# Gated linear attention, top-1 experts and a dense ELU layer in one kernel: joined weight layouts, dense weights kept in SBUF, another order of the attention loop

## The chip, the cores and the metric

The kernel runs on one core of a Trainium2 chip. The metric is the device time of one execution in microseconds; it is given as the median of several runs. Beside it there is one execution recorded by the profiler, with a time and a span of its own.

## The reference

Three layers follow each other, all in fp32.

```python
y[t] = q[t] @ S[t];  S[t] = alpha[t][:, None] * S[t-1] + outer(k[t], v[t])   # 4 x 8 heads, 768 steps, D = 48
x = y regrouped to (3072, 384)
logits = normalize(x) @ normalize(expert_emb).T / tau
idx, gate = argmax(logits), softmax(logits)[argmax]                         # 8 experts
x = gate * (relu(x @ w1[idx]) @ w2[idx])                                    # 384 -> 1024 -> 384
h = x @ w_in                                                                # 384 -> 2048
out = where(h > 0, h, exp(min(h, 0)) - 1) @ w_out                           # 2048 -> 384
```

## The kernel before

All of it is one program with three stages; the order of the instructions is written out by hand, so each engine executes its queue in the order in which the code issues to it.

**Attention (0 to 196 us)** works on 24 tiles of 128 tokens (six time chunks of four batches). Per tile, `stA` (L304) computes on VectorE a backward scan `R` (L316) and a forward scan `A` (L325), each over 112x517 elements, and on GpSimd the products `Kh` = k times `R` (L321) and `Qh` = q times `A` (L328). `stT` transposes `Kh` on TensorE. `stB` (L343) makes the score matrices in PSUM and masks them on VectorE into `P` (L354, two instructions per tile, PSUM in, SBUF out). `stC` and `stD` are the output and state matmuls, `stG` (L384) takes the state update from PSUM (`G`, L391), `stH` loads and prepares what the next tiles need. The loop in `fast` (L603) runs these stages for different tiles in one pass; `mid` is run between the two scans of `stA`.

Routing goes in groups of four tiles: logits, maximum, one-hot, counts and positions are small VectorE instructions on 128x32 or smaller tiles (`stR1`, `stR2`, `stX`, `gates`), put into lists (`todo`, `urgent`) from which `step(n)` takes n at a time. When a tile's gate is known, `scale_x` (L510) scales its rows on ScalarE and `put` (L518) writes the token number beside them on GpSimd (L522) and scatters them to DRAM (`xs`, one region per expert) with an indirect DMA from GpSimd (L523). In twelve of the tiles one piece of an expert weight is split on the side: the high part `whi` by ScalarE (L175), the remainder `wlo` by VectorE (L178); a remainder that is still due waits in the list `lag` and is issued at the end of a pass. After the loop `ending` handles the last two tiles and groups.

**Experts, `moe1` (196 to 473 us)**: 8 experts of 8 blocks. A block n is 9 matmuls of the first layer (`mm1`, L876, weights w1) and 9 of the second for the block before (`mm2`, L890, weights w2), each with 432 columns and with weights and activations split into high and low parts (three products). VectorE and ScalarE form `hh` (L886) and `hl` (L887) of each block. Blocks 4 to 6 of an expert hold the transposes of the next expert's rows (`turn`, L852; L864 and L866). At block 6 of each expert SP issues `idl` (L930), the copy of that expert's token numbers, element by element, from `xs` to a list in DRAM. Expert weights come in 32 loads of 768 KB, each of three pieces that `split_piece` (L162) splits one at a time, with two raw buffers (`stage`) and a ring of 8 high and 8 low buffers of 128x1536.

Beside this, `moe1` prepares the weights of the dense layer, which arrive as 64-bit patterns. In 32 steps j, one to two blocks apart, `decode` (L205) turns a piece of 384 KB into 128x384 fp32 (three integer instructions on VectorE, L212 to L214, a Square on ScalarE, two on GpSimd), `decode_end` (L221) splits it a step later (ScalarE copy L226, VectorE subtraction L227) and writes both halves to DRAM through SP's queue, and `load_d(j + 2)` (L196, L200) fetches the next-but-one raw piece. In the last two experts `load_dense` (L232) reads the split halves back into the ring.

**Dense layer, `moe2` (473 to 882 us)**: 6 slices of 512 tokens by 16 blocks, 21 matmuls each; VectorE and ScalarE compute the ELU (`mn` L1032, `g` L1035, `gl` L1039) with three blocks of lag, and a scatter from GpSimd (L1061) writes the output.

Of the kernel before, what the change touches and what calls it, by code (L numbers as in the profile page):

```python
# [11 lines left out]
I32 = mybir.dt.int32  # L12
# [27 lines left out]
SLOT = 1536  # L40
XW = DM + 1
# [14 lines left out]
def fused_kernel(ctx, tc, qk, a, v, emb, w1, w2, wi, wo, cst, sel, cols, out):  # L56
# [5 lines left out]
    ring = ctx.enter_context(tc.tile_pool(name="ring", bufs=8))  # L62
    stage = ctx.enter_context(tc.tile_pool(name="stage", bufs=2))
# [76 lines left out]
    wq = []  # L140
    for e in range(E):
        for s in range(2):
            wq.append(("w1", e, s, w1[e, :, s * SLOT:(s + 1) * SLOT]))
        for s in range(2):
            wq.append(("w2", e, s, w2[e, :, s * SLOT:(s + 1) * SLOT]))
    raw, whi, wlo = {}, {}, {}
    nload = [0]

    def load_w(n=1):
        for _ in range(n):  # L150
            if nload[0] < len(wq):
                nm, e, s, src = wq[nload[0]]
                t = stage.tile([128, SLOT], F32, tag="raw", name="raw")
                nc.sync.dma_start(out=t, in_=src)
                raw[nload[0]] = t
                nload[0] += 1

    PIECES = 3
    pieces = [(i, j) for i in range(len(wq)) for j in range(PIECES)]
    npc = [0]  # L160

    def split_piece(lag=None):  # L162

        if npc[0] >= len(pieces):
            return
        i, j = pieces[npc[0]]
        npc[0] += 1
        nm, e, s, _ = wq[i]
        if j == 0:
            whi[nm, e, s] = ring.tile([128, SLOT], F32R, tag="whi", name="whi")  # L170
            wlo[nm, e, s] = ring.tile([128, SLOT], F32R, tag="wlo", name="wlo")
        w = SLOT // PIECES
        sl = slice(j * w, (j + 1) * w)
        h, l, r = whi[nm, e, s], wlo[nm, e, s], raw[i]
        nc.scalar.activation(out=h[:, sl], in_=r[:, sl], func=AF.Copy)  # L175

        def low_part():
            nc.vector.tensor_tensor(l[:, sl], r[:, sl], h[:, sl].bitcast(F32), op=ALU.subtract)  # L178
            if j == PIECES - 1:
                raw.pop(i)  # L180
                if i != AHEAD - 1:
# [10 lines left out]
    d_hi = {nm: dram.tile([128, 4 * SLOT], F32, name=nm + "_hi") for nm in ("wi", "wo")}  # L192
    d_lo = {nm: dram.tile([128, 4 * SLOT], F32, name=nm + "_lo") for nm in ("wi", "wo")}
    dbuf = {}
# [8 lines left out]
    dpart = {}  # L203

    def decode(j, pool):  # L205
        if j >= len(dq):
            return
        w = dbuf.pop(j).bitcast(I32).rearrange("p (n two) -> p n two", two=2)
        lo, hi = w[:, :, 0], w[:, :, 1]
        t = pool.tile([128, HS], I32, name="dt")  # L210
# [8 lines left out]
        dpart[j] = (g, tf)  # L219

    def decode_end(j):  # L221
        if j not in dpart:
            return
        nm, s, _ = dq[j]
        g, tf = dpart.pop(j)
# [12 lines left out]
    def wblk(nm, e, col, n):  # L238
        s, c0 = divmod(col, SLOT)
        return whi[nm, e, s][:, c0:c0 + n], wlo[nm, e, s][:, c0:c0 + n]  # L240
# [19 lines left out]
    def attention():  # L260
        with ExitStack() as st:
# [17 lines left out]
            ones = gp.tile([128, 1], F32, name="ones")  # L279

# [21 lines left out]
            Qh, Kh, Rs = {}, {}, {}  # L302

            def stA(i, mid):  # L304

# [4 lines left out]
                if i >= NT:  # L310
                    mid()
                    return
                al = at.pop(i)
# [12 lines left out]
                step(2)  # L326
# [843 lines left out]
```

## Time and profile before

| what | value |
| --- | --- |
| median of 3 runs | 892.02 us (891.55 to 892.13) |
| the profiled execution, its own time | 883.97 us |
| its span | 882.2 us |
| mean granted TensorE clock | 0.955 |
| TensorE busy | 819.9 us (93%) |
| VectorE busy | 565.3 us (64%) |
| ScalarE busy | 356.5 us (40%) |
| GpSimd busy | 207.8 us (24%) |
| HBM read, written | 81.68 MB, 24.81 MB |

How to read it: busy time is the time in which an engine executes, out of the whole span; a matmul is counted with a modelled end, so a busy TensorE isn't one at its peak. The granted clock is a share of TensorE's full speed. Views that are cut by a stretch of time show where an engine is busy and where it is not; a view of waits names the instruction that ended an idle time, in square brackets or behind an arrow.

### The profile page before, as it was taken

How to read it: one execution, taken by the hardware profiler on the slowest of the kernel's cores; microseconds unless marked ns; L12 is line 12 of the kernel's file. 1: busy time of each engine (PE TensorE's matmuls, PEld its weight loads, DVE VectorE, ACT ScalarE, POOL GpSimd, SP SyncE). 2: the span in 40 equal slices, each digit the busy share in tenths (PEclk: the TensorE clock that was granted, in tenths of full speed). 3: DMA queues.
4: the chain of work that ended last, by engine and by line, in shares of the span. 5: the costliest groups of instructions: out<-in, count | busy, mean ns of one | idle time of the engine just before them, and what ended most of it. 6: DMA issues, size and time to landing. Idle time of an engine off the chain costs nothing.

```text
span 882.2 us, 13140 instructions
## 1 busy us (share of the span) xinstructions
PE 819.9 (93%) x4880; PEld 736.4 (83%) x4880; DVE 565.3 (64%) x1054; ACT 356.5 (40%) x739; POOL 207.8 (24%) x235
## 2 busy tenths in 40 slices
PE   7999888749997988989999999999999999999995
PEld 5888777629986987978988999999999999999995
DVE  7899999935785676867734555555555555555552
ACT  2556654614453454545523333333333333333331
POOL 6435555531233233323431001101100100100102
PEclk7898888978998999999999999999999999999999
DMA  9977795235888778978999000000000000000000
GB/s 265 311 191 192 205 261 158 55 102 184 198 241 189 183 223 208 243 208 209 307 299 214 1 1 10 27 1 9 27 1 9 29 1 4 33 0 1 37 1 36
DMA packets 47554, 107.50 MB, mean 122 GB/s; under 512 B 11880, under 2 KB 26472, under 8 KB 47472
## 3 DMA queue, kind: packets, MB, share of 16 engines
q1 hardware_dynamic: 42096, 84.46, 36.0%
q0 software_dynamic: 5376, 22.04, 7.9%
q8 instruction: 41, 0.67, 0.3%
q14 instruction: 41, 0.34, 0.1%
HBM read 81.68 MB, written 24.81 MB: 121 GB/s over the span
## 4 chain that ended last, share of the span: by engine, by line
PE 62%; DMA 8%; DVE 4%; issue 1%; ACT 1%; SPq 0%; POOLq 0%; POOL 0%; DVEq 0%; ACTq 0%
PE h L1030 22%; PE o L1052 8%; PE o L1050 8%; PE o L1051 8%; DMA wi_lo<-dt 5%; DMA wo_lo<-dt 3%; PE y L897 3%; PE y L896 3%; PE y L898 3%; PE h L881 2%; PE h L883 2%; PE h L882 2%; DVE wlo L178 1%; DVE hl L887 1%; PE t L864 1%
## 5 line engine op out<-in xcount | busy, mean ns | idle before, releaser
L1033 ACT ACTIVATE mn<-mn 128x512 f32<-128x512 f32 x96 | 60.7, 632 | 182.4 <-DVE mn L1032 182.4
L1052 PE MATMUL o<-whi,gl 128*128 128x384 f32 x384 | 129.3, 337 | 0.0
L1050 PE MATMUL o<-whi,gh 128*128 128x384 f32 x384 | 129.3, 337 | 0.0
L1051 PE MATMUL o<-wlo,gh 128*128 128x384 f32 x384 | 129.1, 336 | 0.0
L1030 PE MATMUL h<-xh,whi 128*128 128x512 f32 x288 | 112.5, 391 | 0.6 <-ACT x2T L910 0.6
L1030 PE MATMUL h<-xh,wlo 128*128 128x512 f32 x288 | 113.0, 393 | 0.0
L1039 DVE TENSOR_TENSOR gl<-g,gh 128x512 fp32r<-128x512 f32 x96 | 66.6, 694 | 72.4 <-ACT gh L1038 72.4
L1030 PE MATMUL h<-xl,whi 128*128 128x512 f32 x288 | 112.9, 393 | 0.0
L1035 DVE SCALAR_TENSOR_TENSOR g<-mn,h 128x512 f32<-128x512 f32 x96 | 66.1, 689 | 72.6 <-ACT mn L1033 72.6
L1061 POOL DMA_INDIRECT out_dram<-ob,ids x24 | 23.7, 986 | 363.3 <-DVE gl L1039 243.8
L1038 ACT ACTIVATE gh<-g 128x512 fp32r<-128x512 f32 x96 | 60.7, 632 | 77.8 <-DVE g L1035 77.0
L1032 DVE TENSOR_SCALAR mn<-h 128x512 f32<-128x512 f32 x96 | 66.2, 690 | 37.4 <-PE h L1030 37.1
L896 PE MATMUL y<-hh,whi 128*128 128x432 f32 x192 | 73.3, 382 | 9.8 <-ACT hh L886 7.8
L897 PE MATMUL y<-hl,whi 128*128 128x432 f32 x192 | 71.8, 374 | 7.9 <-DVE hl L887 7.9
L178 DVE TENSOR_TENSOR wlo<-raw,whi 128x512 fp32r<-128x512 f32 x96 | 75.6, 810 | 3.8 <-ACT whi L175 3.8
L217 POOL TENSOR_SCALAR dg<-dg 128x384 f32<-128x384 f32 x32 | 41.4, 1293 | 151.6 <-ACT dg L216 151.6
L1050 PEld LDWEIGHTS o<-whi,gh 128*128 128x128 f32 x384 | 72.1, 188 | 3.9
L1051 PEld LDWEIGHTS o<-wlo,gh 128*128 128x128 f32 x384 | 72.1, 188 | 3.8
L1052 PEld LDWEIGHTS o<-whi,gl 128*128 128x128 f32 x384 | 72.1, 188 | 0.0
L898 PE MATMUL y<-hh,wlo 128*128 128x432 f32 x192 | 70.7, 368 | 0.0
L881 PE MATMUL h<-xh,whi 128*128 128x432 f32 x192 | 70.4, 367 | 0.0
L883 PE MATMUL h<-xh,wlo 128*128 128x432 f32 x192 | 69.9, 364 | 0.0
(205 smaller groups left out, 1542.4 us busy)
## 6 DMA issues: line engine op xcount, KB each, us to landing
raw<-in_w_dram SPq DMA_DIRECT2D x32, 768.0 KB, 5.2
qk<-in_qk_dram SPq DMA_DIRECT2D x24, 448.0 KB, 8.1
vt<-in_v_dram SPq DMA_DIRECT2D x24, 352.0 KB, 6.8
raw<-in_wi_dram SPq DMA_DIRECT2D x16, 384.0 KB, 4.1
raw<-in_wo_dram SPq DMA_DIRECT2D x16, 384.0 KB, 4.6
at<-in_alpha_dram SPq DMA_DIRECT2D x24, 226.2 KB, 7.2
xr<-xs SPq DMA_DIRECT2D x7, 576.0 KB, 11.2
wi_hi<-dg SPq DMA_DIRECT2D x16, 192.0 KB, 5.8
```

The source lines that it names most:

```text
L178: nc.vector.tensor_tensor(l[:, sl], r[:, sl], h[:, sl].bitcast(F32), op=ALU.subtract)
L881: nc.tensor.matmul(ps, wh, xh[:, kk], start=(kk == 0), stop=False)
L883: nc.tensor.matmul(ps, wl, xh[:, kk], start=False, stop=(kk == KD - 1))
L896: nc.tensor.matmul(acc[e][d], wh, hh, start=(f == 0), stop=False)
L897: nc.tensor.matmul(acc[e][d], wh, hl, start=False, stop=False)
L898: nc.tensor.matmul(acc[e][d], wl, hh, start=False, stop=(f == FB - 1))
L1030: nc.tensor.matmul(ps, l, x, start=(n == 0), stop=(n == len(terms) - 1))
L1032: nc.vector.tensor_scalar(mn, ps, 0.0, None, op0=ALU.min)
L1039: nc.vector.tensor_tensor(gl, g, gh.bitcast(F32), op=ALU.subtract)
L1050: nc.tensor.matmul(o_, gh[:, sl], wh, start=(f == 0), stop=False)
L1051: nc.tensor.matmul(o_, gh[:, sl], wl, start=False, stop=False)
L1052: nc.tensor.matmul(o_, gl[:, sl], wh, start=False, stop=(f == M - 1))
```

## The change

1. **One weight layout.** w1 and w2 are interleaved on the host into `w12`, 768 columns for each block of an expert. Raw weights are loaded piece by piece (128x512) into six buffers, and each split of a piece issues one more load. The ring has 4 buffers of each kind instead of 8.
2. **Dense weights stay in SBUF.** `decode` writes into a pool `dense` of 18 tiles of 128x768; `decode_end`, the DRAM tensors and `load_dense` are gone. `split_dense` splits one block of a weight into ring buffers (high part) and `dense` tiles (low part): six pairs in the last blocks of `moe1`, the others in the first pass of `moe2`. `load_d(j + 1)` stands ahead of `decode(j)`.
3. **Buffers.** `xr` has a pool of its own; the split input of `moe2` is held in one tile per 128 rows instead of one for all 384.
4. **Attention's order.** `stA` is taken apart: scan `R`, reciprocal and `Kh` (`stR`), then the two `P` (`stP`; its matmuls, `stS`, go ahead), then the scatter of a tile (`put`), then scan `A` and `Qh` (new `stA`), then `G`, the logits, five routing steps, a weight remainder, seven more routing steps. The token number is written by ScalarE in `scale_x`; a `memset` of one element stands ahead of the scatter on GpSimd. The two chains of `stR1` are interleaved two to one.

The diff, cut to its core:

```diff
-    ring = ctx.enter_context(tc.tile_pool(name="ring", bufs=8))
-    stage = ctx.enter_context(tc.tile_pool(name="stage", bufs=2))
+    ring = ctx.enter_context(tc.tile_pool(name="ring", bufs=4))
+    stage = ctx.enter_context(tc.tile_pool(name="stage", bufs=2 * PIECES))
...
+    pieces = [(e, s, j) for e, s in wq for j in range(PIECES)]
...
+                t = stage.tile([128, PW], F32, tag="raw", name="raw")
+                nc.sync.dma_start(out=t, in_=w12[e, :, s * SLOT + j * PW:s * SLOT + (j + 1) * PW])
...
+            nc.vector.tensor_tensor(l[:, sl], r, h[:, sl].bitcast(F32), op=ALU.subtract)
+            load_w()
...
-    HS = SLOT // 4
+    HS = DM
...
+        d, r = divmod(s * HS, DS)
+        if r == 0:
+            dec[nm, d] = dense.tile([128, DS], I32, tag="wd", name="wd")
+        t = dec[nm, d][:, r:r + HS]
...
-    def decode_end(j):
-        nc.scalar.activation(out=g.bitcast(F32R), in_=tf, func=AF.Copy)
-        nc.vector.tensor_tensor(tf, tf, g, op=ALU.subtract)
-        sl = slice(s * HS, (s + 1) * HS)
-        nc.sync.dma_start(out=d_hi[nm][:, sl], in_=g)
-        nc.sync.dma_start(out=d_lo[nm][:, sl], in_=tf)
-    def load_dense(nm, s):
-        whi[nm, 0, s] = ring.tile([128, SLOT], F32R, tag="whi", name="whi")
-        wlo[nm, 0, s] = ring.tile([128, SLOT], F32R, tag="wlo", name="wlo")
-        nc.gpsimd.dma_start(out=whi[nm, 0, s], in_=d_hi[nm][:, s * SLOT:(s + 1) * SLOT])
-        nc.gpsimd.dma_start(out=wlo[nm, 0, s], in_=d_lo[nm][:, s * SLOT:(s + 1) * SLOT])
...
+    def split_dense(nm, m, dense):
+        if m >= F2 // 128:
+            return
+        s, c0 = divmod(m * DM, SLOT)
+        d, r0 = divmod(m * DM, DS)
+        if c0 == 0:
+            dhi[nm, s] = ring.tile([128, SLOT], F32R, tag="whi" if nm == "wi" else "wlo", name="d" + nm)
+        if r0 == 0:
+            dlo[nm, d] = dense.tile([128, DS], F32R, tag="wd", name="dlo")
+        h, l = dhi[nm, s][:, c0:c0 + DM], dlo[nm, d][:, r0:r0 + DM]
+        r = dec[nm, d][:, r0:r0 + DM].bitcast(F32)
+        nc.scalar.activation(out=h, in_=r, func=AF.Copy)
+        nc.vector.tensor_tensor(l, r, h.bitcast(F32), op=ALU.subtract)
+        if r0 + DM == DS:
+            dec.pop((nm, d))
...
+            def stR(i):
...
                 R = Rs[i] = wk.tile([C2, SW], F32, name="R")
-                A = wk.tile([C2, SW], F32, name="A")
-                nc.vector.tensor_tensor_scan(R[:, ::-1], al[:, ::-1], back[:, ::-1], 0.0, op0=ALU.mult, op1=ALU.max)
-                fo = fore[i % 2]
-                nc.vector.reciprocal(seg(fo)[:, :, 0:1], seg(R)[:, :, 1:2])
-                x = qkt.pop(i)
+                nc.vector.tensor_tensor_scan(R[:, ::-1], at[i][:, ::-1], back[:, ::-1], 0.0, op0=ALU.mult, op1=ALU.max)
+                nc.vector.reciprocal(seg(fore[i % 2])[:, :, 0:1], seg(R)[:, :, 1:2])
                 Kh[i] = wk.tile([C2, NP, T], F32, name="Kh")
-                nc.gpsimd.tensor_tensor(Kh[i], x[:, 1], R[:, 1:].rearrange("c (p t) -> c p t", t=TP)[:, :, 1:], op=ALU.mult)
-                step(2)
-                if i < NT - 2:
-                    mid()
-                nc.vector.tensor_tensor_scan(A, al, fo, 0.0, op0=ALU.mult, op1=ALU.add)
-                step(2)
+                nc.gpsimd.tensor_tensor(Kh[i], qkt[i][:, 1], R[:, 1:].rearrange("c (p t) -> c p t", t=TP)[:, :, 1:], op=ALU.mult)
...
+            def stA(i):
...
+                A = As[i] = wk.tile([C2, SW], F32, name="A")
+                nc.vector.tensor_tensor_scan(A, at.pop(i), fore[i % 2], 0.0, op0=ALU.mult, op1=ALU.add)
                 Qh[i] = wk.tile([C2, NP, T], F32, bufs=3, name="Qh")
-                nc.gpsimd.tensor_tensor(Qh[i], x[:, 0], seg(A)[:, :, 1:], op=ALU.mult)
-                nc.scalar.activation(out=chk[:, i], in_=seg(A)[:, :, 0:TP:T], func=AF.Copy)
-                if i >= NT - 2:
-                    mid()
+                nc.gpsimd.tensor_tensor(Qh[i], qkt.pop(i)[:, 0], seg(A)[:, :, 1:], op=ALU.mult)
...
+            def stP(i):
...
+                for h2, s in enumerate(sc.pop(i)):
+                    nc.vector.tensor_tensor(P[i][:, h2], s, c["tri"][:, None, :].to_broadcast([128, NP, T]), op=ALU.mult)
...
+                nc.scalar.activation(out=x[:, DM:], in_=c["tok"][:, i:i + 1], func=AF.Copy)
...
-                nc.gpsimd.tensor_copy(x[:, DM:], c["tok"][:, i:i + 1])
+                if apart and puts:
+                    nc.gpsimd.memset(tick, 0.0)
...
+                    stS(i + 1)
                     stT(i + 1)
-                    def mid():
...
-                    stA(i + 2, mid)
-                    if putq and i >= tail - 2:
+                    stR(i + 2)
+                    stP(i + 1)
+                    if putq and place[putq[0]][0] in gated:
                         put(putq.pop(0))
-                    stB(i + 1)
+                    stA(i + 2)
+                    stG(i - 1)
+                    while late:
+                        late.pop(0)()
+                    if i - 2 in last:
+                        m, n = stR1(last[i - 2])
+                        k = len(m) // 2
+                        todo.extend([f for x in zip(m[::2], m[1::2], n[:k]) for f in x] + n[k:])
+                    while urgent:
+                        urgent.pop(0)()
+                    step(5)
+                    for f in lag:
+                        f()
+                    lag.clear()
+                    step(7)
                     if i == 2:
                         stD(0)
                     if i > 1:
                         stD(i - 1)
+                    stE(i + 2)
                     stC(i)
...
-                xr = stage.tile([128, 4, DM], F32, tag="raw", name="xr0")
+                xr = xr_p.tile([128, 4, DM], F32, name="xr")
...
             load_d(0, dc)
-            load_d(1, dc)
-            load_w()
             load_x(1)
...
                     mm2(*blocks[n - LAG])
-                    e, f = blocks[n - LAG]
-                    if e >= E - 2 and f in (4, 7):
-                        load_dense("wi" if e == E - 2 else "wo", 2 + (f == 7))
-                if n < len(blocks):
-                    e, f = blocks[n]
-                    if e >= E - 2 and f in (4, 7):
-                        load_dense("wi" if e == E - 2 else "wo", f == 7)
-                split_piece()
-                if n % 2:
+                if n > 2:
                     split_piece()
+                    if n % 2:
+                        split_piece()
                 j = (n - 2) * 4 // 7
                 if j >= 0 and j != (n - 3) * 4 // 7:
-                    decode_end(j - 1)
-                    decode(j, dc)
-                    load_d(j + 2, dc)
+                    load_d(j + 1, dc)
+                    decode(j, dc, dense)
+                if n > len(blocks) - 4:
+                    split_dense("wi", n - len(blocks) + 3, dense)
+                    if n > len(blocks) - 2:
+                        split_dense("wo", n - len(blocks) + 1, dense)
...
+                    if u == 0:
+                        split_dense("wi", m + 4, dense)
+                        split_dense("wo", m + 2, dense)
...
+            dense = es.enter_context(tc.tile_pool(name="dense", bufs=18))
```

## Rows read from the trace of the kernel before

**Rows 1.** Windows: stretch, length; busy (count) of PE, PEld, DVE, ACT, POOL; clock, DMA, GB/s.

```profile
196.00:473.40 277.40, 259.07 (x1260) 236.68 (x1260) 181.13 (x309) 126.90 (x254) 81.88 (x79) 0.96 0.83 219
473.40:882.20 408.80, 399.61 (x2016) 363.20 (x2016) 213.20 (x318) 134.96 (x221) 28.92 (x50) 1.00 0.06 20
```

**Rows 2.** Waits of TensorE, 196 to 474: who, on whom; total us, times, longest.

```profile
PE y L897 <- DVE hl L887: 7.9, 8, 1.7
PE y L896 <- ACT hh L886: 7.8, 4, 4.3
PE y L896 <- ACT x2T L906: 2.0, 1, 2.0
```

**Rows 3.** Timeline of TensorE, first matmul of three blocks: start, duration, instruction.

```profile
256.93 0.36 PE L881 MATMUL h<-xh,whi 128*128 128x432 f32 x1
...
261.18 0.36 PE L881 MATMUL h<-xh,whi 128*128 128x432 f32 x1
...
264.71 0.36 PE L881 MATMUL h<-xh,whi 128*128 128x432 f32 x1
```

**Rows 4.** Groups of VectorE, 196 to 474: busy us, mean ns | idle before, releasers.

```profile
L227 DVE TENSOR_TENSOR dt<-dt,dg 128x384 f32<-128x384 f32 x32 | 18.2, 570 | 1.3 <-ACT dg L226 1.2
L212 DVE TENSOR_SCALAR dt<-raw 128x384 int32<-128x384 int32 x32 | 16.0, 501 | 37.3 <-DMA wi_lo<-dt 18.8 <-DMA wo_lo<-dt 18.5
```

**Rows 5.** Timeline of VectorE, 277 to 280; in brackets the idle time before.

```profile
277.45 0.36 DVE L212 TENSOR_SCALAR dt<-raw 128x384 int32<-128x384 int32 x1 [6.76 <-DMA wi_lo<-dt]
...
279.10 0.60 DVE L887 SCALAR_TENSOR_TENSOR hl<-h,hh 128x432 fp32r<-128x432 f32 x1
```

**Rows 6.** Timeline of SP's issues, two of `idl` and the load behind each.

```profile
261.24 0.58 SPq L930 DMA_DIRECT2D idl<-xs  x1
267.82 0.33 SPq L200 DMA_DIRECT2D raw<-in_wi_dram  x1
...
297.31 0.58 SPq L930 DMA_DIRECT2D idl<-xs  x1
302.15 0.33 SPq L200 DMA_DIRECT2D raw<-in_wi_dram  x1
```

**Rows 7.** DMA view: issues at 267.82 and 302.15, us to landing; last, all of L200.

```profile
raw<-in_wi_dram SPq DMA_DIRECT2D x1, 384.0 KB, 10.4
...
raw<-in_wi_dram SPq DMA_DIRECT2D x1, 384.0 KB, 8.8
...
DMA to landing us min/median/max: 3.0/4.5/11.0
```

**Rows 8.** Timeline of VectorE and GpSimd, 100 to 131.

```profile
100.55 1.22 DVE L316 TENSOR_TENSOR_SCAN R<-at,back 112x517 f32<-112x517 f32 x1
...
102.51 1.67 DVE L325 TENSOR_TENSOR_SCAN A<-at,fore 112x517 f32<-112x517 f32 x1
...
104.99 1.73 DVE L461 TENSOR_TENSOR lg<-lg,mx 128x32 f32<-128x32 f32 x1
...
130.84 1.22 DVE L316 TENSOR_TENSOR_SCAN R<-at,back 112x517 f32<-112x517 f32 x1
...
101.90 1.18 POOL L321 TENSOR_TENSOR Kh<-qk,R 112x512 f32<-112x512 f32 x1 [1.84 <-DVE R L316]
...
104.43 1.02 POOL L523 DMA_INDIRECT xs<-xt,pos_i  x1 [0.28 <-DVE mx L459]
105.47 1.19 POOL L328 TENSOR_TENSOR Qh<-qk,A 112x512 f32<-112x512 f32 x1
```

**Rows 9.** Timeline of VectorE at the start of `moe2`.

```profile
479.30 0.69 DVE L1032 TENSOR_SCALAR mn<-h 128x512 f32<-128x512 f32 x1
...
482.68 0.69 DVE L1032 TENSOR_SCALAR mn<-h 128x512 f32<-128x512 f32 x1
```

**Rows 10.** Timeline of GpSimd and VectorE, 159 to 164.

```profile
159.33 1.71 POOL L523 DMA_INDIRECT xs<-xt,pos_i  x1 [1.55 <-DVE P L354]
...
160.53 2.82 DVE L325 TENSOR_TENSOR_SCAN A<-at,fore 112x517 f32<-112x517 f32 x1
```

More of the change, by code (lines that the diff above doesn't have):

```diff
@@ L40 @@
 SLOT = 1536
+PIECES = 3
+PW = SLOT // PIECES
+FW = 2 * DM
+DS = 2 * DM
 XW = DM + 1
@@ L137, in inv_norm1 @@
         return y, steps
[L140 to L145, printed above, removed]
+    wq = [(e, s) for e in range(E) for s in range(FB * FW // SLOT)]
+    pieces = [(e, s, j) for e, s in wq for j in range(PIECES)]
     raw, whi, wlo = {}, {}, {}
     nload = [0]
+    npc = [0]
     def load_w(n=1):
         for _ in range(n):
[L151 to L154, printed above, removed]
+            if nload[0] < len(pieces):
+                e, s, j = pieces[nload[0]]
+                t = stage.tile([128, PW], F32, tag="raw", name="raw")
+                nc.sync.dma_start(out=t, in_=w12[e, :, s * SLOT + j * PW:s * SLOT + (j + 1) * PW])
                 raw[nload[0]] = t
                 nload[0] += 1
-    PIECES = 3
-    pieces = [(i, j) for i in range(len(wq)) for j in range(PIECES)]
-    npc = [0]
     def split_piece(lag=None):
@@ L279, in attention @@
             ones = gp.tile([128, 1], F32, name="ones")
+            tick = gp.tile([1, 1], F32, name="tick")
             qkt, at = {}, {}
@@ L625, in fast @@
                 nc.gpsimd.memset(zero, 0.0)
-                stA(0, lambda: None)
-                stH(0)
-                stA(1, lambda: None)
-                stH(1)
+                for j in range(2):
+                    stR(j)
+                    stA(j)
+                    stE(j)
+                    stH(j)
                 rows, rtau = emb_t[:, :2 * NP * HP], emb_t[:, 2 * NP * HP:]
@@ L686, in fast @@
                         scale_x(putq[0])
-                    for f in lag:
-                        f()
-                    lag.clear()
-                    step(2)
                     for g in [g for j, g in last.items() if i == min(j + 4, tail - 1) and j < tail - 2]:
@@ L834, in pack, with moe1 @@
         ]
-    def moe1(x2T, xr0, t0):
+    def moe1(x2T, xr0, t0, dense):
         with ExitStack() as st:
-            xr_p = st.enter_context(tc.tile_pool(name="xr", bufs=1))
             xT_p = st.enter_context(tc.tile_pool(name="xT", bufs=2))
@@ L904, in mm2 @@
                         for nm in ("xh2", "xl2"):
-                            first.append(stage.tile([128, KD, U], F32R, tag="raw", name=nm))
+                            first.append([stage.tile([128, U], F32R, tag="raw", name=nm) for _ in range(KD)])
                     nc.scalar.activation(out=x2T[:, 0, bass.ds(o1, CAP)], in_=y[0], func=AF.Copy)
@@ L996, in overflow, with moe2 @@
                             for f in range(FB):
-                                o_ = (f * KD + d) * 128
-                                nc.tensor.matmul(t, v2[:, o_:o_ + 128], h[:, f], start=(f == 0), stop=(f == FB - 1))
+                                o_ = f * FW + DM + d * 128
+                                nc.tensor.matmul(t, w[:, o_:o_ + 128], h[:, f], start=(f == 0), stop=(f == FB - 1))
                             nc.vector.tensor_copy(x2T[:, d, bass.ds(col, 128)], t)
-    def moe2(x2T, first):
+    def moe2(x2T, first, dense):
         with ExitStack() as st:
-            x_p = st.enter_context(tc.tile_pool(name="x2", bufs=1))
+            x_p = st.enter_context(tc.tile_pool(name="x2", bufs=KD))
             e_p = st.enter_context(tc.tile_pool(name="el", bufs=2))
@@ L1014, in load_u @@
                 if u % 2:
-                    xh, xl = (x_p.tile([128, KD, U], F32R, tag=nm, name=nm) for nm in ("xh2", "xl2"))
+                    xh, xl = ([x_p.tile([128, U], F32R, tag=nm, name=nm) for _ in range(KD)] for nm in ("xh2", "xl2"))
                 else:
-                    xh, xl = (stage.tile([128, KD, U], F32R, tag="raw", name=nm) for nm in ("xh2", "xl2"))
+                    xh, xl = ([stage.tile([128, U], F32R, tag="raw", name=nm) for _ in range(KD)] for nm in ("xh2", "xl2"))
                 for kk in range(KD):
@@ L1086, in fused_kernel @@
     psG = shared.enter_context(tc.tile_pool(name="psG", bufs=3, space=PS))
+    xr_p = shared.enter_context(tc.tile_pool(name="xr", bufs=1, side="right"))
     x0 = attention()
-    with tc.tile_pool(name="x2T", bufs=1) as p:
+    with tc.tile_pool(name="x2T", bufs=1) as p, ExitStack() as es:
         x2T = p.tile([128, KD, N + CAP], F32, name="x2T")
@@ L1094, in fused_kernel @@
         with tc.manual_schedule():
-            first = moe1(x2T, *x0)
+            dense = es.enter_context(tc.tile_pool(name="dense", bufs=18))
+            first = moe1(x2T, *x0, dense)
             shared.close()
-            moe2(x2T, first)
+            moe2(x2T, first, dense)
 _OUTS = [((N, DM), "float32")]
```

116 lines of the change are left out of this document (51 added, 65 removed).

## The prediction, made before the changed kernel was run

> **What bounds the kernel now.** I read the busy times by stage first. From 473.4 us on (second dense layer pair, "moe2") TensorE is busy 399.6 of 408.8 us at full clock, 4.16 us for each of 96 blocks: nothing but its own work bounds it [rows 1]. From 196.0 to 473.4 us (experts, "moe1") TensorE has less than that to do: 277.4 us, mean granted clock 0.96 [rows 1]. The view of TensorE's waits in that stretch gives 7.9 us for `hl`, 7.8 us for `hh` and 2.0 us for ScalarE's copy into `x2T`, 17.7 us together, the longest 4.3 [rows 2]. The clock is not full either: 0.04 of 277.4 us is 11 us of missing clock at the lower of the two levels. A part of it belongs to the start of the stage, the rest follows the holes; I put half, some 6 us, with the holes. A moe1 without holes would thus be 24 us shorter.
>
> Whose holes they are, the groups of VectorE say: `decode` (L212) sat idle 37.3 us until a write of the decoded dense weights to DRAM had landed [rows 4]. At 277.45 it had waited 6.76 us; `hl`, which TensorE needs, is the next but two on VectorE and ended at 279.70, 2.3 us after the landing [rows 5].
>
> Why writes are late, the queue of SP and the landings say: 261.24 is the issue of `idl` (the token numbers of one expert, element by element), and the load of dense weights issued at 267.82, 6.6 us behind it, took 10.4 us: it landed 17.0 us after the `idl` issue. The same pair at 297.31 and 302.15 landed after 13.6 us (8.8 us of its own) [rows 6, 7]. The median of such a load is 4.5 us, the shortest 3.0 [rows 7]. So every `idl`, one per expert, makes the transfers that follow it land late.
>
> In attention VectorE is busy almost without a gap, but much of that is waiting inside instructions. In the tile from 100.55 to 108.58 the scan `A` (L325) took 1.67 us with `Kh` beside it on GpSimd, against 1.22 for the scan `R`, and a 128x32 subtraction (L461) took 1.73 us: it ended only when GpSimd's indirect DMA and `Qh`, 104.43 to 106.66, were done [rows 8].
>
> **Part 1, dense weights stay in SBUF.** `decode_end`, its 64 writes and the 8 reloads of `load_dense` go; the 37.3 us of waiting for writes, the same wait of ScalarE on `dg`, and with them all holes traced to them: -24 us. What is late next? The load of raw dense weights. Before, `load_d(j+2)` stood behind `decode(j)`; now `load_d(j+1)` stands just ahead of `decode(j)`, one step ahead instead of two, and decodes come 2, 2, 2, 1 blocks apart. A block is 18 matmuls, 3.53 us from 261.18 to 264.71, and 4.25 with transposes in it, from 256.93 [rows 3]. `hl` of block n+1 is due five half blocks after the start S(n) of block n, 9.0 us; less the 2.3 us above [rows 5], a load may land at S(n)+6.7 without a hole. With T the issue of `idl` (block 6 of an expert, S+1.8), the load issued behind it lands at T+13.6 to T+17.0 in the trace of before [rows 6, 7]. Both include traffic that goes: ahead of the load at 302.15 stood two of the 192 KB writes. So I take a little less than the lower, T+12.5; as bounds T+9 and T+15. Then:
> - blocks 6, 30, 46: load two blocks ahead, limit T+12.7: 0;
> - blocks 14 to 16: the load is issued in 15, needed in 16, limit T+12.7, landing about T+13.7: 1 us;
> - block 22: load behind `idl`, needed in block 23, limit T+9.1: 3.4 us;
> - block 29: issued just ahead of `idl`, needed in 30: 0 to 3 us, 1.5 taken.
>
> Sum 6 us, and 2 us of low clock after the longer hole (6 us went with 17.7 us of holes above): 8 us come back. Part 1 is worth -16 us; bounds -24 (T+9, all land in time) and, with T+15, when the five sites lose 2.5 us more each and some clock, about -6.
>
> The 84 weight pieces now load in 256 KB instead of 768 KB with six buffers: a buffer is needed again after four blocks, 15 us, longer than a landing behind `idl`; cost 0, cover 2 us at T+13. The new `xr` buffer makes `load_x(1)` wait for the transposes of expert 0; before it was already stuck on SP behind a weight load until then, cost 0.
>
> **Part 2, the splits move to moe2.** 26 of 32 pairs move into its first 14 blocks. VectorE's period there is 3.38 us from one `mn` to the next; two more subtractions of 0.57 us [rows 4], overlapped by some 0.1 each, make 4.3 [rows 9], against TensorE's 4.16 [rows 1]. It slips 0.15 us a block for 12 blocks, and at block 8 the three splits of the next input cost it 2 us more: some 4 us. The order with three blocks of lag gives about 3 us of cover. +1 us; bounds 0 and +4. ScalarE's two copies run beside `gl`; cost 0.
>
> **Part 3, attention.** `Kh` now runs beside the two PSUM products `P`, so the scan `A` no longer meets it: -0.45 us in a tile like the one shown. The copy of the token number leaves GpSimd (a one-element `memset` stands in its place) and becomes one more small ScalarE instruction, off the path except in the last two tiles (+0.4 us). But the indirect DMA now follows `Kh` and so meets the scan `A`. The nearest rows: at 159.33 an indirect DMA beside the scan `R` took 1.71 us instead of 1.02, which is 0.8 us past the end of the scan, and the scan `A` behind it, asked at 160.53, took 2.82 us [rows 10]. So after `A` there come 0.8 us of indirect DMA and 1.19 of `Qh`; only `G` and `lg` read PSUM beside them, some 0.7 us by the 0.69 of `mn`, which is a little larger than `G` [rows 9]. The routing steps and the weight remainders, which need SBUF alone, wait 1.3 us in the 13 tiles with a scatter, 0.5 in the others. Built up so, a scatter tile is 5.9 us (scan `R` 1.2, reciprocal 0.2, two `P` of the size of `mn` 1.3, scan `A` 1.2, rest of the indirect DMA 0.8, `Qh` 1.2) plus its steps: about 8.1, 8.9, 6.9 and 7.0 us for a group of four, 30.9, against 30.3 before (the scan `R` at 100.55 to the one four tiles later at 130.84 [rows 8]). The second half of a routing chain is now a row of dependent steps with no large instruction between; I put a few hundredths on each. The 13 scatter tiles lose 2 us, the tiles ahead gain 2 to 4. Scatters begin one tile later, so one more falls into the ending, 1.5 us on GpSimd; TensorE stands there waiting for branches until 196 us, which hides it. Sum -1 us; bounds -12 (the indirect DMA loses nothing to the scan) and +8 (the memset holds it until the scan is done, 0.5 us in 13 tiles).
>
> At this place a rule differs. The row has the indirect DMA lengthened by a scan with two SBUF inputs [rows 10]. The Trainium skill, SBUF — State Buffer, section "Who interferes with whom", says that the shared port pair is an exclusive lock, that two SBUF inputs on VectorE contend only with GpSimd instructions that read SBUF, and infers that they don't hold up descriptor generation. The trace agrees with the lock and not with the inference; by the inference the scatters would cost nothing beside `A`, which is the second rival.
>
> **The sum.** -16 +1 -1 = -16 us. The profiled execution took 883.97 us (span 882.2), so 868 there. The median of the runs is 892.02, 8 us above it; which stage holds these 8 us no row tells. I carry the difference over: 876 us.
>
> **The rivals.**
> 1. The jam shrinks with the traffic: loads land by T+9 to T+12 and no hole comes back. For it: many of the transfers behind `idl` are the ones removed. Against: the load of `xr` and `idl` stay. Time 876 - 8 = 868.
> 2. The scatter runs beside the scan: 0.8 us in 13 tiles, -10 us: 866. Against it: the one row above.
> 3. Slower: the one-step-ahead load. The five sites lose five times the excess over T+12.5, and about 1 us of low clock each. At T+15.5 that is 8 + 15 + 5 us, more than the 24 gained; at T+17.0, which the trace has once, 8 + 22.5 + 5 = 35: 892 - 24 + 35 = 903. It decides from about T+15 on. For it: the row at 267.82; against: that load, too, shared the queues with writes that are gone.
> 4. Attention does not gain and its loads come late: a weight piece is now queued on SP in each of 12 tiles, behind the remainder's instruction, and the next tile's inputs stand behind it, one tile ahead instead of two; with the memset's hold +8 to +10 us: 885.
>
> **How the numbers follow.** Forecast (holes partly come back) 0.48, own range 867 to 885; rival 1 0.24; rival 2 0.12; rival 4 0.08; rival 3 0.08. The range has to hold the first two rivals with their bounds and rival 4: 859 to 888. This kernel's measurement can tell 0.2%, 1.8 us, from no change; faster by more than that takes the forecast, rivals 1 and 2 and most of rival 4, 0.88; within 0.2% what is left of it, 0.04; slower rival 3, 0.08.
>
> **What would show it.** In moe1 of the changed kernel: no wait of L212's successor on a write; instead waits of ScalarE's Square or VectorE's first decode step on the raw dense load, longest in block 23; TensorE's waits 5 to 10 us instead of 17.7; the stage 258 to 265 us long. In moe2: waits of TensorE for `gl` in the first pass, under 4 us. In attention: the scan `A` at some 1.2 us in nearly all tiles, `P` no longer than `mn` [rows 9], but the first routing step or remainder after `lg` lengthened to 1 us or more. The forecast is wrong if no instruction in moe1 waits for a raw dense load (rival 1), or if the indirect DMA beside the scan takes 1.0 us (rival 2).

## The result, and the profile after

The changed kernel took 901.15 us, the median of six runs, against 891.91 us for the kernel before on the same chip: the ratio is 1.0101, 95% interval 1.0071 to 1.0131. It is slower by 1%, where the prediction had 876 us and a range up to 888. On a second chip the ratio was 1.0144 (1.0090 to 1.0199, run `e5_changed` below).

The stages show where the time went. The view is the windows of the changed kernel, one row for attention, one for `moe1` and one for `moe2`; the columns are those of [rows 1].

```profile
0.00:205.40 205.40, 155.31 (x1604) 132.35 (x1605) 164.16 (x428) 96.43 (x289) 88.49 (x106) 0.87 0.66 192
205.40:480.80 275.40, 256.84 (x1260) 235.41 (x1260) 168.99 (x281) 114.77 (x226) 75.00 (x65) 0.96 0.57 137
480.80:896.30 415.50, 401.59 (x2016) 362.96 (x2016) 225.64 (x346) 146.57 (x249) 28.07 (x47) 0.99 0.03 12
```

Before, the stages ended at 196.0, 473.4 and 882.2 us. So attention lost 9.4 us, `moe1` won 2.0 where 16 were forecast, and `moe2` lost 6.7 where 1 was forecast: 14.1 us from one profiled span to the other. The profile of the kernel before (883.97 us) is not one of its six runs on this chip, which took 890.13 to 893.92, and the record does not say that it was taken there; where both kernels have a profile on one chip (`e5_changed`, `e7_before`) the stages differ by +12.3, -2.1 and +6.9 us. DMA moved less in `moe1` (137 GB/s against 219 in [rows 1]); that the transfers went is plain, and that it helped so little is the puzzle.

**Attention.** The waits of ScalarE, TensorE and VectorE in the stage (who, on whom; us in total, times, longest), the first lines of each engine's list:

```profile
ACT xt L432 <- DMA xs<-xt,pos_i: 46.7, 12, 7.6
...
PE psX L419 <- ACT yT L376: 16.4, 10, 4.7
...
DVE P L358 <- PE psS L351: 13.1, 8, 4.0
```

None of the three was over 1.1 us in all in the kernel before. They are one chain, and the timeline of one tile (start, duration, instruction; in brackets the idle time before) shows how it runs:

```profile
159.25 0.49 ACT L432 ACTIVATE xt<-psX 128x384 f32<-128x384 f32 x1 [4.06 <-DMA xs<-xt,pos_i]
...
160.40 0.57 ACT L376 ACTIVATE yT<-psY 128x512 f32<-128x512 f32 x1
...
161.02 2.04 PE L419 MATMUL psX<-rhsX,yT 128*128 128x104 f32 x8 [2.12 <-ACT yT L376]
162.85 1.95 PE L371 MATMUL psY<-Qh,G 112*128 112x128 f32 x8
164.74 1.98 PE L374 MATMUL psY<-P,vt 128*64 128x128 f32 x16
166.64 1.34 PE L351 MATMUL psS<-Qh,Kh 48*128 48x128 f32 x16
...
168.01 1.29 DVE L358 TENSOR_TENSOR P<-psS,cs 128x512 f32<-128x512 f32 x2 [3.82 <-PE psS L351]
```

ScalarE copies a tile's rows out of PSUM into a row buffer `xt`. There are eight of these. It waits 4.06 us until a scatter has landed, which reads from the buffer that is to be reused. `yT` stands behind it on ScalarE, the matmuls on `yT` stand in TensorE's queue ahead of the scores `psS` of the next tile, and VectorE's `P` waits 3.82 us for those. After TensorE's idle time its granted clock stood at the lower of its two levels, 1.2 GHz, until the scores began (windows, columns of [rows 1]; the second row is the next tile):

```profile
161.02:166.60 5.58, 5.58 (x32) 5.07 (x32) 2.87 (x8) 1.78 (x7) 3.49 (x3) 0.50 0.10 35
168.84:171.90 3.06, 3.06 (x34) 2.77 (x35) 2.99 (x8) 1.66 (x6) 1.09 (x2) 1.00 0.15 46
```

So `psX` and the first group of `psY` took 2.04 and 1.95 us, where the next tile's took 1.14 and 1.08: a part of what VectorE waits for is clock.

**`moe1`.** TensorE's waits, to be read beside [rows 2]:

```profile
PE y L904 <- ACT hh L894: 8.1, 4, 3.0
PE y L904 <- ACT x2T L914: 5.9, 1, 5.9
PE y L905 <- DVE hl L895: 3.9, 6, 0.8
```

They add up to 17.9 us, as before (17.7). What the engines ahead of it wait for has changed. The groups of VectorE and of ScalarE for the first decode instruction and the Square (busy, mean ns | idle before, releasers), beside [rows 4]:

```profile
L210 DVE TENSOR_SCALAR wd<-raw 128x384 int32<-128x384 int32 x32 | 16.7, 521 | 33.0 <-DMA raw<-in_wi_dram 17.8 <-DMA raw<-in_wo_dram 15.0 <-issue 0.2
...
L214 ACT ACTIVATE dg<-raw 128x384 f32<-128x384 f32 x32 | 17.6, 550 | 45.3 <-DMA raw<-in_wi_dram 23.0 <-DMA raw<-in_wo_dram 22.3
```

The write is gone and the raw load is the late one. SP's queue and the landing of the load issued at 309.20, beside [rows 6, 7]:

```profile
306.25 0.59 SPq L936 DMA_DIRECT2D idl<-xs  x1
309.20 0.42 SPq L196 DMA_DIRECT2D raw<-in_wi_dram  x1
...
raw<-in_wi_dram SPq DMA_DIRECT2D x1, 384.0 KB, 13.0
```

That is 309.20 + 13.0 - 306.25 = 16.0 us behind the issue of `idl`. VectorE's timeline has the other end of it, and TensorE's the hole of 5.93 us that followed, ended by a ScalarE copy that stood behind the Square:

```profile
322.21 0.36 DVE L210 TENSOR_SCALAR wd<-raw 128x384 int32<-128x384 int32 x1 [9.09 <-DMA raw<-in_wi_dram]
...
323.70 0.73 PE L904 MATMUL y<-hh,whi 128*128 128x432 f32 x1 [5.93 <-ACT x2T L914]
```

**`moe2`.** TensorE had no hole in the first slice before. Now it has one, at 563.37, and a smaller one of 0.86 us at 527.77. VectorE's timeline shows one of the blocks with two remainders (L231), TensorE's and ScalarE's the hole:

```profile
487.40 0.55 DVE L231 TENSOR_TENSOR dlo<-wd,dwo 128x384 fp32r<-128x384 f32 x1
487.87 0.68 DVE L1034 TENSOR_SCALAR mn<-h 128x512 f32<-128x512 f32 x1
...
492.19 0.68 DVE L1034 TENSOR_SCALAR mn<-h 128x512 f32<-128x512 f32 x1
...
563.37 0.69 PE L1052 MATMUL o<-dwo,gh 128*128 128x384 f32 x1 [5.06 <-ACT ob L1060]
...
562.31 0.63 ACT L1040 ACTIVATE gh<-g 128x512 fp32r<-128x512 f32 x1 [0.81 <-DVE g L1037]
562.85 0.85 ACT L1060 ACTIVATE ob<-o 128x384 f32<-128x384 f32 x2
```

VectorE's period is 4.32 us here (492.19 - 487.87) and up to 4.44 in the blocks behind it, against TensorE's 4.16. At the end of the slice the evictions `ob` stand in the queues of ScalarE and VectorE behind the late ELU work, and the first matmul of the next slice into those accumulators waits for them.

### The profile page after: what moved, and what is told of

The parts are those of the page before. It is cut to its first block, busy times and chain, and to the rows that moved or that the text cites. A ratio compares the mean times of both kernels' runs of the same rounds, so it can differ in the third digit from the quotient of the medians.

```text
span 896.3 us, 13063 instructions
## 1 busy us (share of the span) xinstructions
PE 813.7 (91%) x4880; PEld 730.7 (82%) x4880; DVE 558.8 (62%) x1054; ACT 357.8 (40%) x763; POOL 191.6 (21%) x218
## 4 chain that ended last, share of the span: by engine, by line
PE 61%; DMA 6%; DVE 5%; ACT 2%; issue 1%; SPq 0%; POOLq 0%; POOL 0%; ACTq 0%; DVEq 0%
PE h L1032 20%; PE o L1054 7%; PE o L1052 7%; PE o L1053 7%; PE y L904 3%; PE y L905 3%; PE y L906 3%; PE h L889 3%; PE h L891 3%; PE h L890 3%; DMA raw<-in_wo_dram 3%; DMA raw<-in_wi_dram 3%; DMA raw<-in_w_dram 1%; PE t L872 1%; DVE g L1037 1%; ACT gh L1040 1%
## 5 line engine op out<-in xcount | busy, mean ns | idle before, releaser
L1052 PE MATMUL o<-dwo,gh 128*128 128x384 f32 x384 | 129.2, 336 | 5.9 <-ACT ob L1060 5.1
L1054 PE MATMUL o<-dwo,gl 128*128 128x384 f32 x384 | 130.0, 339 | 0.1
L1053 PE MATMUL o<-dlo,gh 128*128 128x384 f32 x384 | 129.0, 336 | 0.0
L1032 PE MATMUL h<-xh,dwi 128*128 128x512 f32 x288 | 112.8, 392 | 0.6 <-ACT x2T L918 0.6
L1032 PE MATMUL h<-xh,dlo 128*128 128x512 f32 x288 | 113.2, 393 | 0.0
L1032 PE MATMUL h<-xl,dwi 128*128 128x512 f32 x288 | 112.6, 392 | 0.0
L1052 PEld LDWEIGHTS o<-dwo,gh 128*128 128x128 f32 x384 | 72.5, 189 | 10.9 <-ACT ob L1060 5.5
L175 DVE TENSOR_TENSOR wlo<-raw,whi 128x512 fp32r<-128x512 f32 x96 | 73.4, 788 | 4.9 <-ACT whi L172 4.8
L1053 PEld LDWEIGHTS o<-dlo,gh 128*128 128x128 f32 x384 | 72.4, 189 | 3.9
L895 DVE SCALAR_TENSOR_TENSOR hl<-h,hh 128x432 fp32r<-128x432 f32 x64 | 38.7, 604 | 58.0 <-ACT hh L894 58.0
L1054 PEld LDWEIGHTS o<-dwo,gl 128*128 128x128 f32 x384 | 72.6, 189 | 1.4 <-DVE gl L1041 1.4
```

Source lines behind the costliest of these rows:

```text
L175: nc.vector.tensor_tensor(l[:, sl], r, h[:, sl].bitcast(F32), op=ALU.subtract)
L1032: nc.tensor.matmul(ps, l, x, start=(n == 0), stop=(n == len(terms) - 1))
L1052: nc.tensor.matmul(o_, gh[:, sl], wh, start=(f == 0), stop=False)
L1053: nc.tensor.matmul(o_, gh[:, sl], wl, start=False, stop=False)
L1054: nc.tensor.matmul(o_, gl[:, sl], wh, start=False, stop=(f == M - 1))
```

## The experiments

Eleven runs on three chips. Compared are stages of one chip's runs, or ratios to the kernel before on that chip; only chip 2 has profiles of the kernel before and of the changed kernel, so that on chips 1 and 3 only ratios compare a run with the kernel before, and its stages are set beside those of the other runs there. The attention stage is taken up to the first transposes of expert 0, `moe2` from its first matmul.

| run | attention | moe1 | moe2 | ratio to before (95%) |
| --- | --- | --- | --- | --- |
| chip 1: `e1_ten_rows` | 193.1 | 267.7 | 415.7 | 0.9993 (0.9964 to 1.0023) |
| `e2_two_ahead` | 207.2 | 250.8 | 416.5 | 0.9976 (0.9950 to 1.0002) |
| `e3_lists_later` | 209.2 | 249.8 | 415.8 | 0.9957 (0.9930 to 0.9983) |
| `e4_gpsimd_remainder` | 209.6 | 269.0 | 408.4 | 1.0074 (1.0043 to 1.0106) |
| chip 2: `e5_changed` | 210.5 | 269.3 | 415.7 | 1.0144 (1.0090 to 1.0199) |
| `e7_before` | 198.2 | 271.3 | 408.8 | 1.0001 (0.9967 to 1.0036) |
| `e6_three` | 198.9 | 249.7 | 408.6 | 0.9738 (0.9698 to 0.9778) |
| `e8_scatter_last` | 191.8 | 249.6 | 408.7 | 0.9684 (0.9631 to 0.9736) |
| chip 3: `e9_weights_spread` | 191.0 | 251.0 | 410.3 | 0.9696 (0.9658 to 0.9733) |
| `e10_both_remainders` | 190.9 | 249.7 | 406.4 | 0.9638 (0.9593 to 0.9683) |
| `e11_nine_rows` | 193.6 | 250.9 | 410.2 | 0.9713 (0.9657 to 0.9769) |

### Ten row buffers

```diff
-            xp = st.enter_context(tc.tile_pool(name="xp", bufs=8))
+            xp = st.enter_context(tc.tile_pool(name="xp", bufs=10))
```

> The changed kernel with one size altered: ten row buffers (xt) in attention instead of eight. Theory A, a row buffer that comes free only when its scatter has landed stalls ScalarE's copy out of PSUM, and through yT, TensorE and the scores VectorE too: ScalarE's 46.7 us of waiting for scatters in attention fall under 5, VectorE's 13.1 us of waiting for scores under 6, the first transposes of the experts start at 196 to 199 us instead of 205.4, and the time falls by 6 to 9 us. Rival, the order itself (the scatter beside the scan, the later input loads) costs the 9.4 us: ScalarE's waits go but the transposes still start at 203 or later, time within 2 us of the changed kernel.

ScalarE's wait on scatters for L432 is gone; on its list of waits 0.8 us is left on any scatter. Attention ended at 193.1 us, 14 to 16.5 us ahead of the three runs beside it. VectorE's wait for scores fell only to 9.1 us, more than expected: a part of it has another cause, for TensorE's scores waited 11.6 us for `Qh` there, seven times; what that costs was not tried by itself. Theory A stands, and its size was put too low. The rival falls by its own sign: the transposes started ten us ahead of its 203. Attention is now 5 us shorter than in `e7_before`, but on another chip.

### Raw loads two steps ahead

```diff
             load_d(0, dc)
+            load_d(1, dc)
...
-                    load_d(j + 1, dc)
                     decode(j, dc, dense)
+                    load_d(j + 2, dc)
```

> The changed kernel with the raw dense loads two steps ahead again: load 1 beside load 0, and load j+2 behind decode j. Theory B, the distance of one step is what lets landings behind the token-number copies hold TensorE: its waits in moe1 fall from 17.9 us to under 5, the stage from 275 to 256 to 260 us, the time by 14 to 18 us. Rival, the jam is longer than two steps as well or other waits take its place: waits of 10 us or more stay, the time falls by less than 7 us.

The windows row of `moe1`:

```profile
207.20:458.00 250.80, 250.16 (x1261) 233.00 (x1261) 169.06 (x281) 115.66 (x226) 73.44 (x65) 0.98 0.62 149
```

TensorE is busy 250.2 of 250.8 us; the only wait left is one of 0.6 us at the seam to `moe2`. Against 269.0 us in `e4_gpsimd_remainder` on the same chip that is 18 us, and the stage is 5 us shorter than the 256 expected. One step of distance was the whole of the loss, although `idl` stands where it stood.

### Token-number copies later

```diff
-                    if f == 6:
-                        o3 = nc.sync.value_load(off_i[0:1, e:e + 1], min_val=0, max_val=N)
-                        nc.sync.dma_start(out=idl[bass.ds(o3, CAP)], in_=xs[e * REG:e * REG + CAP, DM:])
...
+            for e in range(E):
+                o3 = nc.sync.value_load(off_i[0:1, e:e + 1], min_val=0, max_val=N)
+                nc.sync.dma_start(out=idl[bass.ds(o3, CAP)], in_=xs[e * REG:e * REG + CAP, DM:])
             nc.sync.dma_start(out=idf, in_=idl[0:N].rearrange("(t p) o -> p (t o)", p=128))
```

> The changed kernel with the eight copies of token numbers (idl) issued at the start of moe2 instead of at block 6 of each expert; the loads stay one step ahead. Theory C, the jam behind those copies is what makes the loads late: with it gone raw dense loads land in 3 to 5 us, TensorE's waits in moe1 fall under 5 us, the stage to 256 to 260 us, the time by 14 to 18 us, unless the list comes too late for the first output rows. Rival, one step is too short even without the jam: waits of 8 us or more stay.

`moe1` took 249.8 us with the loads still one step ahead, 6 us less than expected. The raw loads' median was 4.0 us; the longest took 9.8, over the expected 5, and held no matmul. So the holes need both, the jam behind `idl` and the short distance; taking away either ends them. The list at the start of `moe2` came in time: that stage is as long as in the runs beside it.

### Remainders of one weight on GpSimd

```diff
-        nc.vector.tensor_tensor(l, r, h.bitcast(F32), op=ALU.subtract)
+        (nc.vector if nm == "wi" or m < 2 else nc.gpsimd).tensor_tensor(l, r, h.bitcast(F32), op=ALU.subtract)
```

> The changed kernel with the remainders of the second dense weight (14 of the 26 made in moe2) computed on GpSimd instead of VectorE. Theory D, VectorE's two extra subtractions per block make it fall behind until the evictions of the first slice hold TensorE: the holes of 5.1 and 0.9 us in moe2 fall under 1, the stage from 415.5 to 409 to 410 us, the time by 5 to 7 us. Rival, the same work on GpSimd takes VectorE's memory port and slows it as much: holes of 3 us or more stay, time within 3 us of the changed kernel.

`moe2` fell from 415.7 to 408.4 us. The hole at the turn of the slice is 1.7 us, over the expected 1:

```profile
PE o L1052 <- ACT ob L1060: 1.7, 1, 1.7
```

### The changed kernel, the kernel before, and the three edits together

The first two are the kernels as they stand; `e6_three` has the edits of `e1`, `e2` and `e4`.

> The changed kernel as it is, for its stages beside those of the next runs. All theories: about 1% above the kernel before, attention until some 205 to 210 us, moe1 268 to 276 us, moe2 415 us.

> The changed kernel with three edits together: ten row buffers, raw dense loads two steps ahead, the second dense weight's remainders on GpSimd. If the three losses are separate (they lie in three stages that follow each other): attention 193 to 197 us, moe1 250 to 252 us, moe2 408 to 409 us, a span near 853, 3.5 to 4.5% below the changed kernel and 2.5 to 3.5% below the one before. Rival, what one stage gains comes back in the next (later loads, a colder clock): the sum falls short by 5 us or more.

> The kernel before as it is, for its stages on the same chip. Attention until some 196 to 200 us, moe1 270 to 278 us, moe2 409 us. If ten row buffers only took back what the new order had lost, its attention is no longer than that of the run with three edits; if the new order itself gains, it is 2 us longer or more.

On this chip the changed kernel differs from the one before in the same way by stage (attention +12.3, `moe1` -2.1, `moe2` +6.9 us), and the edits together take back both losses but for 0.7 us of attention, and win 21.6 us in `moe1`: 895.4 to 857.2 us of span, 4% below the changed kernel, 2.6% below the one before. `moe1` and `moe2` came out as expected. Attention is 2 us over the top of what was expected, no shorter than before; 4.4 us of it is a wait of ScalarE in the ending that the trace puts on no engine of this core, which `e1_ten_rows` did not have (`e5_changed` had one of 3.1). So whether the new order alone gains anything isn't settled by these two runs.

### Scatter behind scan A and Qh

```diff
                     stP(i + 1)
-                    if putq and place[putq[0]][0] in gated:
-                        put(putq.pop(0))
                     stA(i + 2)
+                    if putq and place[putq[0]][0] in gated:
+                        put(putq.pop(0))
                     stG(i - 1)
```

> The three edits, and the scatter of a tile put behind scan A and Qh instead of ahead of them. Theory E, the scatter that meets the scan A (1.85 us instead of 1.01) and then holds Qh costs each of 13 tiles 0.5 to 0.8 us: scatters take 1.0 us, attention is 4 to 8 us shorter than with the three edits. Rival, the routing steps are held by Qh and the scatter just as long, or the later scatter makes ScalarE wait for row buffers again: attention within 2 us, or longer.

Attention fell by 7.1 us, from 198.9 to 191.8. GpSimd's and VectorE's timelines around one scatter, first with ten rows alone (`e1_ten_rows`):

```profile
105.50 1.85 POOL L528 DMA_INDIRECT xs<-xt,pos_i  x1 [0.15 <-issue]
107.37 1.20 POOL L323 TENSOR_TENSOR Qh<-qk,A 112x512 f32<-112x512 f32 x1
...
105.30 1.22 DVE L321 TENSOR_TENSOR_SCAN A<-at,fore 112x517 f32<-112x517 f32 x1
...
107.39 1.24 DVE L463 TENSOR_TENSOR e__1382<-lg,mx 128x32 f32<-128x32 f32 x1
```

and then behind the scan (`e8_scatter_last`):

```profile
103.98 1.19 POOL L323 TENSOR_TENSOR Qh<-qk,A 112x512 f32<-112x512 f32 x1 [1.61 <-DVE A L321]
...
105.36 1.01 POOL L528 DMA_INDIRECT xs<-xt,pos_i  x1 [0.16 <-issue]
...
104.70 0.52 DVE L463 TENSOR_TENSOR e__1382<-lg,mx 128x32 f32<-128x32 f32 x1
```

Beside the scan the scatter takes 1.85 us and ends 0.83 after it; `Qh` follows, and the first routing step (L463) waits inside itself until `Qh` is done (108.6). Behind the scan, `Qh` starts at once, the scatter takes 1.01 us, and the same routing step takes 0.52: it too ends with `Qh`, which is done earlier. With this order attention is 6.4 us shorter than in `e7_before` on the same chip.

A scatter beside the scan was not always slow. In `e1_ten_rows` nine of the 13 scatters of the loop began after the scan (0.2 to 1.1 us) and took 1.73 to 1.88 us, ending 0.8 to 1.0 after it; four began up to 0.5 us ahead of it or together with it and took 1.01, and the scan 1.23 to 1.28. The kernel before had three of the second kind beside `A`. One of them from each, with the scan beside it, first of `e1_ten_rows`, then of the kernel before:

```profile
113.10 1.01 POOL L528 DMA_INDIRECT xs<-xt,pos_i  x1 [0.16 <-issue]
113.52 1.23 DVE L321 TENSOR_TENSOR_SCAN A<-at,fore 112x517 f32<-112x517 f32 x1
...
119.55 1.02 POOL L523 DMA_INDIRECT xs<-xt,pos_i  x1 [0.28 <-POOL xt L522]
119.72 1.22 DVE L325 TENSOR_TENSOR_SCAN A<-at,fore 112x517 f32<-112x517 f32 x1
```

### Weight pieces spread, both remainders on GpSimd, nine rows

All three start from `e8_scatter_last`.

```diff
-                    if i == 1:
-                        load_w(2 * PIECES)
+                    if 1 <= i < 6:
+                        load_w(2 if i == 1 else 1)
```

> The run with the scatter put last (ten rows, two steps ahead, GpSimd remainders), and the six first weight pieces requested two in pass 1 and one in each of passes 2 to 5, instead of six in pass 1. Theory F, six requests in a row (3.8 us on SP) ahead of the next tile's inputs are what loses some 5 to 6 us in the first eight tiles against the kernel before: the scan R of tile 8 starts at 50 to 52 us instead of 55, attention is 3 to 5 us shorter (187 to 189 us), the time falls by as much. Rival, the loss there comes from the new order of TensorE's and GpSimd's work: tile 8 starts at 54 or later and the time is the same.

A miss: the scan `R` of tile 8 started at 53.82 us, against 55.09 in `e8_scatter_last` and 48.57 in `e7_before`, and the time did not move (0.9696 against 0.9684). Nor is the start a gain: without the spread it was 54.75 and 53.48 in `e10` and `e11` on the same chip. The 5 to 6 us that the first eight tiles lose against the kernel before lie elsewhere. In that stretch VectorE's `P` still waited 3.8 us once for scores, and TensorE, ahead of them, 2.7 us for VectorE's `lg`, which frees the PSUM of `psX`. Whether that is the cause was not tried.

```diff
-        (nc.vector if nm == "wi" or m < 2 else nc.gpsimd).tensor_tensor(...)
+        (nc.vector if m < (4 if nm == "wi" else 2) else nc.gpsimd).tensor_tensor(...)
```

> The run with the scatter put last, and the remainders of both dense weights in moe2 on GpSimd. Theory D, VectorE's own work per block decides: with none of them the wait of 2.0 us that is left in moe2 falls under 0.5, the stage from 408.7 to 406 to 407 us. Rival, two subtractions a block on GpSimd hold VectorE's gl at the shared port: the wait is 2 us or more, the stage 408 to 412.

No wait of TensorE is left in `moe2`, and the stage is 406.4 us. `e9` and `e11`, with VectorE's share, took 410.3 and 410.2 on the same chip. This is the fastest version: 849.91 us, ratio 0.9638 (0.9593 to 0.9683) to the kernel before, though the interval overlaps that of `e8`, on another chip.

`e11_nine_rows` has `bufs=9` where `e8` has 10.

> The run with the scatter put last, with nine row buffers instead of ten. If the scatter's delay of one tile is all that eight buffers lacked, nine do: ScalarE waits for scatters under 5 us in attention, which ends within 2 us of 192. Rival, the landing takes longer than one tile: waits of 10 to 30 us and an attention 4 us longer or more.

In between: ScalarE still waited 19.8 us for scatters, eight times, but attention ended at 193.6, 2 to 3 us later than in the runs beside it. So a buffer is held for longer than one more tile. One buffer more than eight takes most of the loss, two all of it (nine were run only with the scatter behind the scan).

## Why the prediction was wrong

**Attention, forecast -1, measured +9.4.** The scan `A` came out as forecast, 1.22 to 1.24 us in 23 of 24 tiles. The scatter beside it did not: in the changed kernel eight of the 13 scatters of the loop took 1.01 us, seven of them begun when the scan was over, and five took 1.27 to 2.00. What was priced shows only where the wait for buffers is gone (`e1_ten_rows`, 1.85 us in most tiles, with the routing step held by `Qh`). The failed step is that only the engines' time of the scatter was moved one tile later, and not what the scatter holds: the row buffer that it reads. "Scatters begin one tile later, so one more falls into the ending" is the sentence; the same delay keeps each of the eight row buffers a tile longer, and the instruction that next writes that buffer is on ScalarE, ahead of the work that TensorE and then VectorE need. Two more buffers gave 14 to 16.5 us back. The fourth rival did look for a slower attention, and its +8 to +10 us hold the +9.4, but by luck: it had the input loads and the `memset`. `e9_weights_spread` shows no gain from moving the weight requests, and the `memset` took 0.09 us each time. The cover was wrong too: TensorE's waiting for branches does not hide a longer ending. It is 9.0 us in the changed kernel and 9.6 in the one before, and it begins when the ending ends.

The second rival, a scatter that runs beside the scan at no cost, is out for the order as it was built: most scatters of `e1_ten_rows` took 1.85 us, and between the two orders (`e6_three`, `e8_scatter_last`) lie 7 us of stage. But the prediction went by one row, and the same trace had three where the scatter began 0.2 us ahead of the scan and cost nothing: which of the two begins first was left out. The Trainium skill, SBUF — State Buffer, section "Who interferes with whom", infers that `tensor_tensor`, also with both inputs in SBUF, does not hold up descriptor generation. The runs speak against it: nine scatters of `e1_ten_rows` that began inside the scan, which has two inputs in SBUF too, took 1.73 to 1.88 us, and in `e8_scatter_last` the two that began 0.2 us into a `tensor_tensor` (`wlo`, L175, at 93.33 and 119.24) took 1.35 and 1.34 and ended 0.9 after it.

**`moe1`, forecast -16, measured -2.0.** The mechanism was right: with the writes gone the raw load, one step ahead, became the late one, behind the copies. The mis-sized term is the landing behind `idl`, taken as 12.5 us on the ground that much traffic goes. Measured were 14.8 to 16.6 us at six of the eight copies (16.0 at the one shown). With these the forecast's own limits hold: at its five sites the landings of 14.8, 16.4, 16.0, 15.8 and 14.8 us give 2.1, 3.7, 6.9, 3.1 and 2.1 us, and TensorE's holes there were 2.1, 3.5, 5.9, 3.0 and 2.7; 0.6 more came behind a sixth copy, and nothing at block 29. That is 17.9 us, as much as the writes had cost, and the granted clock stayed at 0.96; where the 2.0 us of gain come from isn't shown. The sums around it are rougher. The bound of -6 at T+15 does not follow from its terms: 16 less five times 2.5 is 3.5, before any clock. The third rival had the right cause, but its 903 is near the 901.15 by luck: it has a `moe1` 11 us longer, and the time was lost in the other two stages. DMA had fallen from 219 to 137 GB/s, so the bytes that were removed were not what made the loads late; `e3_lists_later` shows that the element-wise copy was. `e2_two_ahead` gave 250.8 us, 18 below its neighbour, and `e6_three` 249.7, 21.6 below the kernel before on the same chip: most of the 24 us of the sum were there to be had.

**`moe2`, forecast +1, measured +6.7.** VectorE's period was nearly right (4.3 forecast, 4.32 to 4.44 measured), and so was the slip of some 4 us: from the first `mn` to the tenth there are 41.38 us, 3.9 more than nine of TensorE's blocks. The failed step is the cover: "the order with three blocks of lag gives about 3 us". That lag covers `gl`. The evictions of the first slice's accumulators stand behind the same late work, and the next slice needs those accumulators at once. The hole there was 5.06 us, 0.86 came at the first use of `gh`, and the 0.8 left of the 6.7 fit the clock behind the hole (granted 0.77 from 563.4 to 570.0). `e4_gpsimd_remainder` and `e10_both_remainders`, which take work from VectorE, leave 1.7 us and no hole.

**The sum.** -16 + 1 - 1 stood against -2.0 + 6.7 + 9.4 = +14.1 us in the profiled spans. The runs differ by 9 us on the first chip. The median of the kernel before lies 8 us above its profiled time, that of the changed kernel 3, so that carrying a difference from one profile to the runs was good to some 5 us only.

## What to carry to other kernels

When a DMA that reads a buffer is issued later, follow the buffer: find the instruction that writes it next, the engine it stands on, and who waits behind it there; here that was worth more than the price of the moved instruction. Before one row is taken as the price of two instructions side by side, look for every row where they meet, and at which began first. When transfers are removed, do not assume that the ones left land sooner: ask what made them late, and keep the distance of the loads until a trace shows it. Count the cover of a slipping engine at the place that needs it first, here the eviction of an accumulator and not the next product.

## What was not expected of the hardware

An element-wise DMA of 1.7 KB (432 elements of 4 bytes) took 8.0 to 10.7 us to land in the changed kernel (9.1 to 14.5 before), and the load of 384 KB behind it 9.7 to 13.3 us, where the median is 4.2: that load did not land sooner when the traffic beside it fell by more than a third. An indirect DMA that began inside a scan of VectorE ended 0.8 us or more after it; begun first, in `e1_ten_rows` and the kernel before, it took 1.01 to 1.02 us and the scan lost 0.06 at most. GpSimd took 1.0 to 1.1 us for a remainder that takes VectorE 0.55, twice per block, and VectorE's `gl` beside it stayed at 0.69 us. In the ending ScalarE waited 3.1 to 4.5 us in `e5`, `e6` and the runs built on it for something that the trace calls remote; what that is stays open.
